# First routing group of a fused WKV-attention and mixture-of-experts kernel: temporaries in PSUM columns in place of SBUF, the mask of the two chosen experts by one comparison, the gates' products in two operations

## The chip, the cores and the metric

The kernel runs on one core of one Trainium2 chip. The metric is the device time of one execution in microseconds (us); lower is better. The kernel before takes 592.07 us, the median of 3 runs. TensorE is PE below (PEld are its weight loads), VectorE is DVE, ScalarE is ACT, GpSimd is POOL, and SP is the engine that issues most of the DMA transfers.

## The reference, cut to what matters

```python
# attention: r, k, v [4, 8, 768, 48]; a state of 48 x 48 for each head decays by w in each step
y[:, :, t] = einsum('bhd,bhde->bhe', rt, state + einsum('bhd,bhe->bhde', u * kt, vt))
state = w * state + einsum('bhd,bhe->bhde', kt, vt)
# x = y as [3072 tokens, 384]; mixture of experts, E = 8, F = 1024, two experts for each token
noisy = x @ w_gate + log1p(exp(x @ w_noise)) * noise
top2 = the two largest of the 8; top2_w = exp(top2_l - max); top2_w /= top2_w.sum(-1) + 1e-9
for e in range(8):
    mask = tokens that chose e
    out[mask] += top2_w * (relu(x[mask] @ w1[e]) @ w2[e])
```

## The kernel before, in words

The tokens are handled as 24 tiles of 128 (`NT`), tile i holding chunk i // 4 of batch i % 4. The first part of the kernel is a loop over these 24 tiles, `for i in range(NT)`. In each turn PE forms scores and outputs of tile i, DVE masks the next tile's scores (`mask`, L485), multiplies the transposed r by a table of powers (`rT`, L465), updates the state (`zt`, L508) and adds up the output tile x (`xout`, L561). PE then transposes x (L225 into `KX`), and ACT evicts that (`xT`, L471) for the product with the two gate matrices (L574). POOL multiplies k, r and u (L403, L422 and others), updates the state z (L512) and subtracts halves of the first expert's weights (L355, L358). SP issues all loads of r, k, v in order, five tiles ahead.

The second part is the experts, dense on PE: two products for each expert and chunk of tokens (L1136, L1172), with gathers and scatters by POOL.

Between them lies the routing, `route(g)`, once for each of two groups of 12 tiles (`GROUPS`). It computes from the logits `lg` the noise scale by a polynomial exponential (`expneg`) and a polynomial logarithm, finds the largest two of the 8 noisy logits (`m1`, `m2`, one-hot masks `oh`), sums the masks over the tokens by PE (`pr`, L819 to L822, with triangular and all-one matrices) to give each token its place in its expert's list, and builds the first expert's list by one-hot products (`pairs`, `drop`, `place`). The two gate weights come from a second, small `expneg` on the difference of the two logits (`r2` names) and from `gates()`; they are written to the DRAM rows `xd` beside x. All of it but the sums and products is DVE work on tiles of [128, 12, 8] (96 columns) or [128, 12] (12 columns).

The routing is written as generators. The attention loop takes a few of their steps in each turn (`steps(n)`), so that the routing of group 0 (tiles 0 to 11) stands in DVE's program between the attention operations of tiles 13 to 23, and that of group 1 after the loop. [...]

Where temporaries live: `T(name)` is a tile in SBUF. `P(k, shape)` is one of four columns of 96 in a tile `PG[0]`: for group 0 that is the PSUM tile `RT` (one bank of 512 columns), for group 1 the SBUF tile `PS`. `RT` also takes `pr` (columns from 384) and the lists' products (`drop`), and the third tile's transposes at the start of the experts (`xT_first`, columns 0 to 383, L1075), where PE leaves the loop: `xT_first` transposes three gathered tiles and the last x, and ACT and DVE split them into `xh` and `xl` for the first expert's products.

Of the kernel before, what the change touches and what calls it, by code (L numbers as in the profile page):

```python
# [56 lines left out]
def kernel(  # L57
# [14 lines left out]
    nc = tc.nc  # L72
# [513 lines left out]

    def expneg(a, shape, tg, res):

# [5 lines left out]
        r1, sc = T("r"), T("s", I32)  # L594
        t, nm, q = (P(k, shape) for k in (1, 2, 3)) if len(shape) == 3 else (T("t"), res, res)
        nc.vector.tensor_scalar(t, a, -LOG2E, MAGIC, op0=ALU.mult, op1=ALU.add)
# [26 lines left out]

    routed = set()

    def T_of(n):
# [28 lines left out]

    def pairs(g, sli, slf, nm):

        i0, i1 = GROUPS[g]
        shape = list(slf.shape)
        k = shape[1] if len(shape) == 3 else 1  # L660
        T = T_of(i1 - i0)
        ej = T(nm + "j", shape, I32)
        mm2, ej2 = T(nm + "m2", shape + [2], BF16), T(nm + "e2", shape + [2], BF16)
        nc.vector.tensor_single_scalar(ej, sli, 7, op=ALU.logical_shift_right)
        yield
        dup = [list(mm2.shape)] * 2
        ejb = (ej[:, :, None] if k == 1 else ej[:, :, :, None]).to_broadcast(dup[0])
        slb = (slf[:, :, None] if k == 1 else slf[:, :, :, None]).to_broadcast(dup[0])
        nc.vector.tensor_copy(ej2, ejb)
        yield  # L670
        nc.vector.scalar_tensor_tensor(mm2, ejb, -128.0, slb, op0=ALU.mult, op1=ALU.add)
        yield mm2, ej2
# [60 lines left out]

    GATES, list0 = {}, []

    def route(g, lists=True, behind=iter(())):
# [17 lines left out]
        for j, _ in enumerate(expneg(a, sh, "r1", ee)):  # L754
# [3 lines left out]
            yield  # L758
        d = rtp[0].tile([128, GB * E], F32, name="r1r", bufs=1)[:, :n * E].rearrange("p (a b) -> p a b", b=E)
        s, s2, q, nl, sn = T("s"), T("s2"), P(2, sh), T("nl"), T("sn")  # L760
# [22 lines left out]
        OHS[g] = oh  # L783
        da, e2 = T("da", [128, n]), T("e2", [128, n])
        if lists:
            m1, m2, nl2 = T("m1", [128, n, 1]), T("m2", [128, n, 1]), T("zp")
            nc.vector.tensor_reduce(m1, nl, AX.X, ALU.max)
# [8 lines left out]
            yield  # L796
            nc.vector.tensor_sub(da, m1[:, :, 0], m2[:, :, 0])
            yield
        else:
# [7 lines left out]
            nc.vector.tensor_sub(da, m8[:, :, 0], m8[:, :, 1])  # L807
        nc.vector.tensor_scalar(da, da, 87.0, None, op0=ALU.min)
        ex = expneg(da, [128, n], "r2", e2)
        yield  # L810
        om = T("om", dt=BF16)
        nc.vector.tensor_add(om, oh[:, 0], oh[:, 1])
        sm = rtp[0].tile([128, E, 1], F32, name="r_sm", bufs=1)
        yield
        nc.vector.tensor_reduce(sm, om.rearrange("p j e -> p e j"), AX.X, ALU.add)
        yield "pe"

        pr = RT[:, 4 * GB * E:(4 * GB + n) * E].rearrange("p (a b) -> p a b", b=E)
        nc.tensor.matmul(pr, ltri, om, start=True, stop=False, skip_group_check=True)  # L819
# [48 lines left out]
        if lists:  # L868
            s0, s0i = T("s0", [128, n]), T("s0i", [128, n], I32)
            nc.vector.scalar_tensor_tensor(s0, slf[:, :, 0], 1.0, om[:, :, 0], op0=ALU.add, op1=ALU.mult)  # L870
            yield
            nc.vector.tensor_scalar(s0i, s0, -1.0, None, op0=ALU.add)
            yield
            for c in pairs(g, s0i, s0i, "p"):
                yield 0.2
# [789 lines left out]
```

## Time and profile before

| | |
|---|---|
| runs | 592.07 us median of 3 (589.45, 592.07, 592.11) |
| profiled execution | 594.45 us, of which span of the instructions 592.3 us |
| PE busy | 570.7 us, 96% |
| DVE busy | 346.8 us, 59% |
| ACT busy | 284.8 us, 48% |
| POOL busy | 282.0 us, 48% |
| mean granted clock of PE | 0.991 |

The table is of one profiled execution; its time is 2.1 us more than its span, which is outside of the instructions. The shares are averages over two parts of the kernel: the attention loop lasts until about 127 us, the experts from there to the end.

### The profile page before, as it was taken

What the parts mean: (1) busy time and instruction counts of PE and PEld (TensorE: products, weight loads), DVE (VectorE), ACT (ScalarE), POOL (GpSimd) and SP (SyncE); (2) the same over time, 40 slices, a digit from 0 to 9 for tenths busy, and PEclk for the clock granted to TensorE, in tenths of its full rate; (3) what the DMA queues carried; (4) which work ended last, traced back from release to release, by engine and by line L of the source; (5) the groups of instructions that cost most, each with busy time, mean ns of one, the idle gap of its engine ahead of it and who ended that gap; (6) DMA issues with size and microseconds to landing.
All of it is one profiled execution on the core that took longest, in us unless ns stands there. A gap on an engine that the chain in (4) does not pass through costs nothing.

```text
span 592.3 us, 13907 instructions
## 1 busy us (share of the span) xinstructions
PE 570.7 (96%) x5383; PEld 544.7 (92%) x5384; DVE 346.8 (59%) x781; ACT 284.8 (48%) x714; POOL 282.0 (48%) x420
## 2 busy tenths in 40 slices
PE   8999989979979999999999999999999999999995
PEld 5899979869979999999999999999999999999995
DVE  7988889778745444546455645555464546454331
ACT  4348877832343443554445554455454454445220
POOL 8997767720426443436345443444353436333222
PEclk9999999989989999999999999999999999999998
DMA  8998999167504643675655646455756555424211
GB/s 162 196 210 190 232 224 233 54 168 225 157 2 140 208 145 92 177 181 146 122 166 142 191 107 185 120 178 111 177 132 152 150 149 171 128 92 85 66 35 42
DMA packets 143225, 86.53 MB, mean 146 GB/s; under 512 B 118624, under 2 KB 133215, under 8 KB 143152
## 3 DMA queue, kind: packets, MB, share of 16 engines
q1 hardware_dynamic: 132368, 56.76, 40.2%
q0 software_dynamic: 10160, 28.81, 16.3%
q8 instruction: 44, 0.72, 0.5%
q14 instruction: 29, 0.24, 0.1%
q10 hardware_dynamic: 624, 0.00, 0.1%
HBM read 58.81 MB, written 19.86 MB: 133 GB/s over the span
## 4 chain that ended last, share of the span: by engine, by line
PE 80%; DVE 7%; POOL 6%; issue 3%; ACT 2%; DMA 1%; another core or an unknown queue 1%; POOLq 0%; DVEq 0%; ACTq 0%
PE ph L1136 36%; PE pym L1172 33%; POOL kd L403 2%; PE pym L1165 2%; PE pym L1163 2%; POOL rku L411 2%; PE py L532 2%; DVE am L485 1%; POOL rku L415 1%; PE PAB L477 1%; DVE x L561 1%; PE KX L225 1%; DVE rT L465 1%; PE RT L714 1%; PE ptm L1054 1%
## 5 line engine op out<-in xcount | busy, mean ns | idle before, releaser
L1172 PE MATMUL pym<-w1h,hb 128*128 128x384 f32 x768 | 200.2, 337 | 0.0
L1142 DVE SCALAR_TENSOR_TENSOR hb<-ph,hb 128x384 fp32r<-128x384 f32 x128 | 71.2, 557 | 119.7 <-ACT ht L1140 73.6
L1172 PEld LDWEIGHTS pym<-w1h,hb 128*128 128x128 f32 x768 | 139.4, 188 | 0.2
L1136 PE MATMUL ph<-xh,w0h 128*128 128x384 f32 (+1 forms) x384 | 136.3, 355 | 0.0
L1136 PE MATMUL ph<-xh,w0l 128*128 128x384 f32 (+1 forms) x384 | 136.2, 355 | 0.0
L1136 PE MATMUL ph<-xl,w0h 128*128 128x384 f32 (+1 forms) x384 | 130.6, 354 | 0.0
L1172 PE MATMUL pym<-w1l,hb 128*128 128x384 f32 x384 | 129.2, 336 | 0.0
L1140 ACT ACTIVATE hb<-ph 128x384 fp32r<-128x384 f32 x128 | 62.9, 492 | 111.2 <-PE ph L1136 106.4
L1197 POOL DMA_INDIRECT out_dram<-ot,TK x56 | 60.0, 1071 | 100.4 <-DVE ot L1191 44.4
L1025 POOL DMA_INDIRECT xg<-xd,GR x56 | 60.9, 1088 | 53.6 <-DVE r_e L608 24.6
L1136 PEld LDWEIGHTS ph<-xh,w0h 128*128 128x128 f32 x384 | 72.9, 190 | 3.7 <-issue 0.2
L1136 PEld LDWEIGHTS ph<-xl,w0h 128*128 128x128 f32 x384 | 72.8, 190 | 3.3
L1136 PEld LDWEIGHTS ph<-xh,w0l 128*128 128x128 f32 x384 | 72.9, 190 | 3.2
L1040 POOL DMA_INDIRECT pv<-out_dram,GA x49 | 50.1, 1022 | 51.0 <-DMA out_dram<-ot,TK 38.6
L1172 PEld LDWEIGHTS pym<-w1l,hb 128*128 128x128 f32 x384 | 72.1, 188 | 0.1
L1110 ACT ACTIVATE xh<-xj 128x384 fp32r<-128x384 f32 (+1 forms) x42 | 21.2, 504 | 43.7 <-DVE xj L1108 38.3
L1180 ACT ACTIVATE ot<-pym 128x384 f32<-128x384 f32 x42 | 20.5, 487 | 41.3 <-PE pym L1172 31.7
L1111 DVE TENSOR_TENSOR xl<-xj,xh 128x384 fp32r<-128x384 f32 (+1 forms) x42 | 22.4, 534 | 24.9 <-ACT xh L1110 18.4
L1096 ACT ACTIVATE pl<-xg 128x768 uint16<-128x768 uint16 (+1 forms) x42 | 35.3, 841 | 1.6 <-DMA xd<-pl 1.5
L485 DVE TENSOR_TENSOR am<-PAB,mneg 128x512 int32<-128x512 int32 x48 | 30.8, 685 | 4.2 <-PE PAB L477 2.8
L454 ACT ACTIVATE cv<-vt,c 128x48 f32<-128x48 f32 x120 | 30.3, 326 | 0.2
L403 POOL TENSOR_TENSOR kd<-kt,tabk 128x192 f32<-128x192 f32 x46 | 28.6, 643 | 3.6 <-PE RV L225 2.4
(275 smaller groups left out, 828.2 us busy)
## 6 DMA issues: line engine op xcount, KB each, us to landing
stg<-in_moe_w_dram SPq DMA_DIRECT2D x24, 512.0 KB
stg<-in_moe_w_dram SPq DMA_DIRECT2D x32, 384.0 KB
xd<-x SPq DMA_DIRECT2D x24, 196.0 KB
rd<-in_r_dram SPq DMA_DIRECT2D x24, 192.0 KB
vt<-in_v_dram SPq DMA_DIRECT2D x24, 192.0 KB
out_dram<-ot SPq DMA_DIRECT2D x16, 288.0 KB
kt<-in_k_dram SPq DMA_DIRECT2D x23, 192.0 KB
xg<-xd,GR POOLq DMA_INDIRECT x56
```

The costliest lines, as they stand in the source:

```text
L403: nc.gpsimd.tensor_mul(KD[i][:, h], kt[i][:, h], tabk[:, h, :D])
L454: nc.scalar.activation(CV[i][:, h, :], vt[i][:, h, :], AF.Copy, scale=C8[i][:, h, :])
L485: nc.vector.tensor_tensor(am[:, :, h].bitcast(I32), pa[:, :, h].bitcast(I32), mneg[:, None].to_broadcast([128, 2, NP // 2, 128]), op=ALU.b ...
L1025: nc.gpsimd.indirect_dma_start(out=xg[:n, :XW if e else DM], out_offset=None, in_=xd[:rows_of(early_)], in_offset=bass.IndirectOffsetOnAxi ...
L1040: nc.gpsimd.indirect_dma_start(out=pv[:n], out_offset=None, in_=out, in_offset=bass.IndirectOffsetOnAxis(ap=GA[:n, e * NJ + t:e * NJ + t + ...
L1096: nc.scalar.activation(pl[:n], XG[e, t][:n, :DM].bitcast(U16).rearrange("p (d two) -> p two d", two=2), AF.Copy)
L1111: nc.vector.tensor_sub(xl, xj, xh.bitcast(F32))
L1136: nc.tensor.matmul(ph[:, :w_], a[:, d, fs], x[:, d, :w_], start=(j == 0), stop=(j == len(q) - 1))
L1140: nc.scalar.activation(h_[:, f, 0, :], ph[:, a:b], AF.Relu)
L1142: nc.vector.scalar_tensor_tensor(h_[:, f, 1, :], ph[:, a:b], 0.0, h_[:, f, 0, :].bitcast(F32), op0=ALU.max, op1=ALU.subtract)
L1172: nc.tensor.matmul(py, hb[:, f, a, hs], x[:, f, :], start=(j == 0), stop=(j == len(q) - 1))
L1197: st = nc.gpsimd.indirect_dma_start(out=out, out_offset=bass.IndirectOffsetOnAxis(ap=TK[:n, q:q + 1], axis=0), in_=ot[:n], in_offset=None, ...
```

## The change: what it does, and the diff

For group 0 alone (`own`), temporaries move from SBUF tiles to columns of the PSUM tile `RT`, through a new helper `V(c, shape)`: the reciprocal `d`, the noisy logits `nl`, the masked logits `nl2`, the difference `d0`, the small exponential's `et` and `e2`, the counts `sm`, the list's `s0`, `ej` and `ej2` (the last in four bytes in place of two). The prefix sums `pr` move to the columns 0 to 95, and `s0` is taken from `pr` itself. The mask of both chosen experts, `om`, is the comparison of `nl` with `m2` in place of the sum of the two one-hot masks. In `gates()` the two gate values are also kept in PSUM, which doubles the reciprocal and the product, and the products with the one-hot masks are two operations of 96 columns in place of one of 192. Group 1 is as before. Nothing else in the kernel is changed.

```diff
-    def expneg(a, shape, tg, res):
+    def expneg(a, shape, tg, res, t=None):
-        t, nm, q = (P(k, shape) for k in (1, 2, 3)) if len(shape) == 3 else (T("t"), res, res)
+        t, nm, q = (P(k, shape) for k in (1, 2, 3)) if len(shape) == 3 else (T("t") if t is None else t, res, res)
...
+    def V(c, shape, dt=F32):
...
+        t = RT[:, c:c + w_]
...
-    def pairs(g, sli, slf, nm):
+    def pairs(g, sli, slf, nm, pv=None):
-        ej = T(nm + "j", shape, I32)
-        mm2, ej2 = T(nm + "m2", shape + [2], BF16), T(nm + "e2", shape + [2], BF16)
+        ej = T(nm + "j", shape, I32) if pv is None else pv[0]
+        mm2 = T(nm + "m2", shape + [2], BF16)
+        ej2 = T(nm + "e2", shape + [2], BF16) if pv is None else V(pv[1], shape + [2])
...
+        own = lists and PG[0] is RT
+        d = P(1, sh) if own else rtp[0].tile(...)
...
+        if own:
+            nl = P(1, sh)
         nc.vector.tensor_add(nl, q, zp)
...
+        d0, e2, et = (V(4 * GB * E + j * GB, [128, n]) for j in range(3)) if own else (da, T("e2", [128, n]), None)
-            m1, m2, nl2 = T("m1", [128, n, 1]), T("m2", [128, n, 1]), T("zp")
+            m1, m2, nl2 = T("m1", [128, n, 1]), T("m2", [128, n, 1]), P(3, sh) if own else T("zp")
...
-            nc.vector.tensor_sub(da, m1[:, :, 0], m2[:, :, 0])
+            nc.vector.tensor_sub(d0, m1[:, :, 0], m2[:, :, 0])
...
-        nc.vector.tensor_scalar(da, da, 87.0, None, op0=ALU.min)
-        ex = expneg(da, [128, n], "r2", e2)
+        nc.vector.tensor_scalar(da, d0, 87.0, None, op0=ALU.min)
+        ex = expneg(da, [128, n], "r2", e2, et)
...
-        nc.vector.tensor_add(om, oh[:, 0], oh[:, 1])
-        sm = rtp[0].tile([128, E, 1], F32, name="r_sm", bufs=1)
+        if own:
+            nc.vector.tensor_tensor(om, nl, m2.to_broadcast(sh), op=ALU.is_ge)
+        else:
+            nc.vector.tensor_add(om, oh[:, 0], oh[:, 1])
+        sm = V(5 * GB * E + E + 2 * E, [128, E, 1]) if own else rtp[0].tile([128, E, 1], F32, name="r_sm", bufs=1)
...
-        pr = RT[:, 4 * GB * E:(4 * GB + n) * E].rearrange("p (a b) -> p a b", b=E)
+        po = 0 if own else 4 * GB * E
+        pr = RT[:, po:po + n * E].rearrange("p (a b) -> p a b", b=E)
...
+            if own:
+                gp = V(4 * GB * E + 2 * GB, [128, 2, n])
+                nc.vector.tensor_scalar(gp[:, 1], e2, 1.0, 1e-9, op0=ALU.add, op1=ALU.add)
+                yield
+                nc.vector.reciprocal(GTS[:, 0, i0:i1], gp[:, 1])
+                nc.vector.reciprocal(gp[:, 0], gp[:, 1])
+                yield
+                nc.vector.tensor_mul(GTS[:, 1, i0:i1], e2, GTS[:, 0, i0:i1])
+                nc.vector.tensor_mul(gp[:, 1], e2, GTS[:, 0, i0:i1])
+                yield
+                bc = [gp[:, kk, :, None].to_broadcast(sh) for kk in range(2)]
+                og, gd = T("os", [128, 2, n, E])[:, 0], T("a")
+                nc.vector.tensor_mul(og, oh[:, 0], bc[0])
+                yield
+                nc.vector.tensor_mul(P(2, sh), oh[:, 1], bc[1])
+                yield
+                nc.vector.tensor_add(gd, og, P(2, sh))
+                nc.sync.dma_start(xd[i0 * 128:i1 * 128, DM:].rearrange("(n p) e -> p n e", p=128), gd)
...
+                s0, s0i, pv = V(so, [128, n]), T("s0i", [128, n], I32), (V(so + GB, [128, n], I32), GB * E)
+                nc.vector.scalar_tensor_tensor(s0, pr[:, :, 0], 1.0, om[:, :, 0], op0=ALU.add, op1=ALU.mult)
```

No instruction changes its place among the others; what the edit moves is three added DVE instructions and some waits. The first place is DVE's program in the turn that follows PE's prefix sums (L596 is the first step of the small exponential, L485 the two halves of the mask of the next tile). Before:

```order
L465 TENSOR_TENSOR rT<-RV,pwr 128x2x4x64 [waits PE_49]
L596 TENSOR_SCALAR r2t<-r_da 128x12
L485 TENSOR_TENSOR am<-PAB,mneg 128x2x256 [waits PE_49]
L485 TENSOR_TENSOR am<-PAB,mneg 128x2x256
L598 TENSOR_SCALAR r_e_2127<-r2t 128x12 [waits DVE_49]
```

The same place of the change:

```order
L465 TENSOR_TENSOR rT<-RV,pwr 128x2x4x64 [waits PE_49]
L596 TENSOR_SCALAR RT<-r_da 128x12 [waits DVE_49,PE_49]
L485 TENSOR_TENSOR am<-PAB,mneg 128x2x256 x2
L598 TENSOR_SCALAR RT<-RT 128x12 [waits DVE_49]
```

L596 now waits for PE, since it writes the bank in which the prefix sums are formed, and the mask behind it has no wait of its own left. The second place is DVE's program at the last tile (x_149 is its x; behind it `gates()` ends, and `xT_first` begins). Before:

```order
L847 TENSOR_SCALAR GTS<-r_e_2127 128x12 [waits DVE_49]
L850 RECIPROCAL GTS<-GTS 128x12 [waits DVE_49]
L852 TENSOR_TENSOR GTS<-r_e_2127,GTS 128x12 [waits DVE_49]
L561 TENSOR_TENSOR x_149<-py,cv 128x384 [waits DMAHW4_49,PE_49,Activation_49]
L856 TENSOR_TENSOR r_os<-OH_242,GTS 128x192 [waits DVE_49]
L859 TENSOR_TENSOR r_a<-r_os 128x96 [waits DVE_49]
```

The same place of the change:

```order
L868 TENSOR_SCALAR RT<-RT 128x12 [waits DVE_49]
L870 RECIPROCAL GTS<-RT 128x12 [waits DVE_49]
L871 RECIPROCAL RT<-RT 128x12
L873 TENSOR_TENSOR GTS<-RT,GTS 128x12 [waits DVE_49]
L874 TENSOR_TENSOR RT<-RT,GTS 128x12
L561 TENSOR_TENSOR x_149<-py,cv 128x384 [waits DMAHW4_49,PE_49,Activation_49]
L878 TENSOR_TENSOR r_os<-OH_242,RT 128x96 [waits DVE_49]
L880 TENSOR_TENSOR RT<-OH_242,RT 128x96 [waits DVE_49]
L882 TENSOR_TENSOR r_a<-r_os,RT 128x96 [waits DVE_49]
```

Two instructions are new ahead of the last x, and one behind it. The third place is PE's program at the same point, the transposes of the third gathered tile into `RT` (L1075 before, L1121 of the change). Before:

```order
L225 MATMUL KX<-ident,x_149 128x64 x5
L1075 MATMUL RT<-ident,xg 128x128 [waits DMASW2_49]
L574 MATMUL pl<-wg,xT 64x64 [waits Activation_49]
```

The same place of the change:

```order
L225 MATMUL KX<-ident,x_149 128x64 x5
L1121 MATMUL RT<-ident,xg 128x128 [waits DMASW2_49,DVE_49]
L574 MATMUL pl<-wg,xT 64x64 [waits Activation_49]
```

The transposes wait for DVE as well now, since the gates' products lie in columns that they overwrite.

## Rows read from the trace of the kernel before

**Rows 1.** The page's first line.

```profile
span 592.3 us, 13907 instructions
```

**Rows 2.** Windows between PE's first product (L532) of one tile and the next.

```profile
core 0: us, PE busy (x) PEld busy (x) DVE busy (x) ACT busy (x) POOL busy (x), PEclk, DMA share, GB/s
...
77.45:82.93 5.48, 4.91 (x133) 4.63 (x131) 5.38 (x14) 3.92 (x13) 3.95 (x6) 1.00 0.81 175
82.93:89.53 6.60, 4.89 (x133) 4.64 (x130) 4.85 (x17) 4.51 (x16) 4.10 (x7) 1.00 0.99 244
89.53:95.31 5.78, 5.47 (x148) 5.12 (x144) 5.75 (x15) 4.30 (x15) 4.05 (x7) 1.00 0.99 230
95.31:100.03 4.72, 4.72 (x132) 4.60 (x130) 3.79 (x10) 3.60 (x13) 3.75 (x6) 1.00 1.05 224
100.03:106.02 5.99, 5.26 (x134) 4.79 (x131) 5.85 (x15) 4.11 (x15) 3.95 (x6) 1.00 0.68 186
106.02:111.25 5.23, 5.10 (x129) 4.67 (x127) 4.83 (x11) 5.08 (x19) 4.78 (x7) 1.00 0.22 80
120.79:127.65 6.86, 4.26 (x97) 3.51 (x93) 5.23 (x14) 4.33 (x15) 2.50 (x3) 1.00 0.40 115
```

**Rows 3.** Timeline of PE: starts, lengths, and the idle time ahead with its releaser.

```profile
82.59 0.40 PE L225 MATMUL KX<-ident,x 64*128 64x64 f32 x6 [0.57 <-DVE x L561]
...
88.07 0.41 PE L225 MATMUL RV<-ident,rd 64*128 64x64 f32 x7 [1.71 <-issue]
...
94.47 0.40 PE L225 MATMUL KX<-ident,x 64*128 64x64 f32 x6 [0.31 <-DVE x L561]
...
95.17 0.20 PE L822 MATMUL RT<-acc,ones_b 128*128 128x96 bf16 x1
...
96.74 0.62 PE L532 MATMUL py<-vt,am 128*64 128x48 f32 x16
...
105.69 0.40 PE L225 MATMUL KX<-ident,x 64*128 64x64 f32 x6 [0.61 <-DVE x L561]
...
125.79 0.40 PE L225 MATMUL KX<-ident,x 64*128 64x64 f32 x6 [1.10 <-DVE x L561]
126.12 0.55 PE L1075 MATMUL RT<-ident,xg 128*128 128x128 f32 x3
```

**Rows 4.** Timeline of DVE in group 0's routing.

```profile
80.38 1.13 DVE L765 TENSOR_TENSOR r_s<-r_nl,r1r 128x96 f32<-128x96 f32 x1
...
81.89 0.55 DVE L561 TENSOR_TENSOR x<-py,cv 128x384 f32<-128x384 f32 x1
...
92.62 0.77 DVE L808 TENSOR_SCALAR r_da<-r_da 128x12 f32<-128x12 f32 x1
...
100.35 0.74 DVE L870 SCALAR_TENSOR_TENSOR r_s<-SLF,r_om 128x12 f32<-128x12 f32 x1
...
123.21 1.15 DVE L608 SCALAR_TENSOR_TENSOR r_e<-r_e,r2r 128x12 f32<-128x12 f32 x2
```

**Rows 5.** Timeline of POOL at the same moments.

```profile
80.11 1.29 POOL L358 TENSOR_TENSOR w0l<-stg,w0h 128x512 fp32r<-128x512 f32 x1
...
92.36 1.00 POOL L358 TENSOR_TENSOR w1l<-stg,w1h 128x384 fp32r<-128x384 f32 x1
```

**Rows 6.** Timeline of DVE in group 1's routing, the same lines with POOL idle.

```profile
134.97 0.26 DVE L765 TENSOR_TENSOR r_s<-r_nl,r1r 128x96 f32<-128x96 f32 x1
...
140.64 0.17 DVE L808 TENSOR_SCALAR r_da<-r_da 128x12 f32<-128x12 f32 x1
```

**Rows 7.** DVE's groups by line and form: the same operation in PSUM and in SBUF.

```profile
L761 DVE TENSOR_SCALAR RT<-r_nl 128x96 f32<-128x96 f32 x1 | 0.3, 261 | 0.0
...
L761 DVE TENSOR_SCALAR PS<-r_nl 128x96 f32<-128x96 f32 x1 | 0.2, 211 | 0.0
```

**Rows 8.** Timeline of DVE at the last tile.

```profile
126.03 0.26 DVE L859 TENSOR_TENSOR r_a<-r_os 128x96 f32<-128x96 f32 x1
```

**Rows 9.** Timeline of ACT at the last tile.

```profile
126.96 0.52 ACT L1080 ACTIVATE xh<-RT 128x384 fp32r<-128x384 f32 x1
```

More of the change, by code (lines that the diff above doesn't have):

```diff
@@ L624 @@
     routed = set()
+    def V(c, shape, dt=F32):
+        w_ = 1
+        for z in shape[1:]:
+            w_ *= z
+        t = RT[:, c:c + w_]
+        t = t if dt == F32 else t.bitcast(dt)
+        ax = "abcd"[:len(shape) - 1]
+        return t if len(shape) == 2 else t.rearrange(f"p ({' '.join(ax)}) -> p {' '.join(ax)}",
+                                                     **dict(zip(ax, shape[1:])))
     def T_of(n):
@@ L732, in rest @@
             yield from drop(g, mm2[:, kk], ej2[:, kk], IJ_REST, (E - 1) * NJ, NJ, g == 0 and kk == 0)
-    GATES, list0 = {}, []
+    GATES, list0, gated = {}, [], []
     def route(g, lists=True, behind=iter(())):
@@ L758, in route @@
             yield
-        d = rtp[0].tile([128, GB * E], F32, name="r1r", bufs=1)[:, :n * E].rearrange("p (a b) -> p a b", b=E)
+        own = lists and PG[0] is RT
+        d = P(1, sh) if own else rtp[0].tile([128, GB * E], F32, name="r1r", bufs=1)[:, :n * E].rearrange(
+            "p (a b) -> p a b", b=E)
         s, s2, q, nl, sn = T("s"), T("s2"), P(2, sh), T("nl"), T("sn")
@@ L783, in route @@
         OHS[g] = oh
-        da, e2 = T("da", [128, n]), T("e2", [128, n])
+        da = T("da", [128, n])
+        d0, e2, et = (V(4 * GB * E + j * GB, [128, n]) for j in range(3)) if own else (da, T("e2", [128, n]), None)
         if lists:
-            m1, m2, nl2 = T("m1", [128, n, 1]), T("m2", [128, n, 1]), T("zp")
+            m1, m2, nl2 = T("m1", [128, n, 1]), T("m2", [128, n, 1]), P(3, sh) if own else T("zp")
             nc.vector.tensor_reduce(m1, nl, AX.X, ALU.max)
@@ L845, in gates @@
                 yield
+            if own:
[16 more added lines that the diff above has]
+                nc.sync.dma_start(xd[i0 * 128:i1 * 128, DM:].rearrange("(n p) e -> p n e", p=128), gd)
+                gated.append(g)
+                yield 0.25
+                return
             dn = GTS[:, 1, i0:i1]
@@ L868, in route @@
         if lists:
-            s0, s0i = T("s0", [128, n]), T("s0i", [128, n], I32)
-            nc.vector.scalar_tensor_tensor(s0, slf[:, :, 0], 1.0, om[:, :, 0], op0=ALU.add, op1=ALU.mult)
+            so = 4 * GB * E + 5 * GB
+            if own:
+                s0, s0i, pv = V(so, [128, n]), T("s0i", [128, n], I32), (V(so + GB, [128, n], I32), GB * E)
+                nc.vector.scalar_tensor_tensor(s0, pr[:, :, 0], 1.0, om[:, :, 0], op0=ALU.add, op1=ALU.mult)
+            else:
+                s0, s0i, pv = T("s0", [128, n]), T("s0i", [128, n], I32), None
+                nc.vector.scalar_tensor_tensor(s0, slf[:, :, 0], 1.0, om[:, :, 0], op0=ALU.add, op1=ALU.mult)
             yield
@@ L873, in route @@
             yield
-            for c in pairs(g, s0i, s0i, "p"):
+            for c in pairs(g, s0i, s0i, "p", pv):
                 yield 0.2
```

## The prediction

> **What bounds the kernel now.** I read the windows first, cut at PE's first product of each tile. The whole span is 592.3 us [rows 1], most of it experts that the edit does not touch. In the attention loop the turn from 95.31 to 100.03 us is one in which PE never waits: span and PE busy are both 4.72 us [rows 2]. I take that as the floor of a turn. The turns around it are longer although they hold the same attention work, and DVE is what is full there: 5.38 of 5.48 us, 5.75 of 5.78, 5.85 of 5.99 [rows 2]. These are the turns in which group 0's routing stands in DVE's program.
>
> Next the timeline of PE: in each of these turns it idles ahead of the transposes of x, and the releaser is DVE's x (L561): 0.57, 0.31 and 0.61 us, and 1.10 us at the last tile [rows 3]. One hole has another cause: 1.71 us at 88.07 us, where PE waited for nothing that the profile shows [rows 3].
>
> Last, DVE's own rows beside POOL's. L765 takes 1.13 us in group 0 [rows 4] and 0.26 us in group 1, where POOL is idle [rows 6]. It starts at 80.38 and ends at 81.51, and POOL's subtraction runs from 80.11 to 81.40 [rows 5]: DVE waits for POOL's operation to end and then does its own 0.2 us. L808 does the same (0.77 against 0.17 us [rows 4, 6]): it ends at 93.39, POOL's operation at 93.36 [rows 5]. So group 0's routing pays for a conflict with POOL, not for work. L765 has two inputs in SBUF; L808 has one, and goes from SBUF to SBUF.
>
> **The change, part by part.** I take it that an operand in PSUM takes such an operation out of the conflict: x (L561), which reads PSUM, takes 0.55 us while POOL works [rows 4]. I go by turns, since a turn can't fall under PE's floor; what DVE saves beyond that is lost. Moved operations that are not named in a turn (L835 and others) save time only where DVE is ahead of PE anyway.
>
> *Turn at 77.45 (L763, L765): 0.2 us.* The excess is 5.48 - 4.72 = 0.76 us, of which PE's wait for x is 0.57. L765 loses its stall of 1.13 - 0.26 = 0.87. But the next operation is s*s (L767), whose inputs stay in SBUF. It would now start at about 80.7, while POOL's subtraction still runs to 81.40 [rows 5], so it waits in place of L765. After it come about 0.26 us for L768 and x, which starts at about 81.65 in place of 81.89 [rows 4]. Bounds: nothing, and 0.57 if L767, which reads one tile twice, is free of the conflict. [...]
>
> *Turn at 89.53 (L791, L795, L808, the new mask): 0.45 us.* The excess over the floor is 5.78 - 4.72 = 1.06; the prefix sums, which stay, are some 0.5 of it (PE busy is 5.47 here), and PE's wait for x is 0.31 [rows 2, 3]. L808's 0.60 us alone is more than that wait. L797 still has two SBUF inputs and can still stall, but it has the rest of L808's and L791's savings to cover it. The comparison that makes the mask reads 96 columns at four bytes and is priced at L765's 0.26 us [rows 6]; x waits for PE's output by then. Bounds 0.31 and 0.56.
>
> *Turn at 95.31: 0.* It is at the floor. Here the new wait of L596 falls: it stands ahead of the mask (L485), and now holds it until the last prefix sum, which ended at 95.37 [rows 3]. Queued behind it are both halves of the mask, for which PE's output products wait; these began at 96.74, 1.37 us after the sums [rows 3]. L596 (12 columns, 0.17 as L808, [rows 6]) and the first half of the mask (I take x's 0.55, the row nearest in width, [rows 4]) need 0.7 to 0.8 with the start, so the cover is half a microsecond. If it were gone, the price would be what the mask comes late, up to the 0.5 that the sums take.
>
> *Turn at 100.03 (L870, L664, L669, L671): 1.15 us.* The excess is 5.99 - 4.72 = 1.27 us, PE's wait for x 0.61 [rows 2, 3]. L870 shows 0.74 us [rows 4] for 12 columns; group 1's 12-column L808 takes 0.17 [rows 6]. L870 stands ahead of the mask and so delays PE a second time. All four operations lose an SBUF input or output. Behind them L692 (two SBUF inputs, one of them the list's mask) stays and can stall once; I leave 0.1 for it. Bounds 0.61 and 1.27.
>
> *Turn at 106.02: 0.4 us.* PE does not wait for DVE's x here, but POOL waits for DVE's rT (L465) and PE for POOL's product. rT comes earlier when x does. Excess 5.23 - 4.72 = 0.51 us, PE idle 5.23 - 5.10 = 0.13 [rows 2]: bounds 0.1 and 0.51.
>
> *Last tile: 0.4 us.* The two steps of L608 ahead of x took 1.15 us [rows 4]. A 12-column operation alone takes 0.17 and a dependent one of 96 columns 0.26 [rows 6]; I take 0.28 for each step, so the pair saves 0.58. The second reciprocal and the second product are new ahead of x; nothing ahead of them holds them, so I charge each half of 0.17, together 0.17. That leaves 0.4 of PE's wait of 1.10 for x [rows 3]. Bounds: 0, and 0.8 (the stall down to two times 0.17, the new ones free). The new wait of L1121: the gates' last operation (L859) ended at 126.29 [rows 8], 0.5 us behind the start of x's transposes at 125.79 [rows 3]. With one operation more in front it is 0.6, the third tile's transposes start there in place of 126.12, take 0.55 [rows 3] and end at 126.94 on this clock; ACT, busy with what stands ahead, reads them at 126.96 [rows 9]. ACT's queue covers it with nothing to spare; without that cover it costs the 0.1 of the added operation.
>
> The move has a price of its own. L761 takes 261 ns into PSUM and 211 into SBUF [rows 7]; some 40 operations of group 0 move, 2.0 us if each costs 50 ns. I take nothing for it, since the turns at 89.53 to 106.02 leave DVE time once the stalls are gone, and the first and the last turn hold few moved operations.
>
> The sum: 0.2 + 0.45 + 1.15 + 0.4 + 0.4 = 2.6 us. Nothing behind 127 us changes except that it starts earlier. The span becomes 592.3 - 2.6 = 589.7, the profiled execution 594.45 - 2.6 = 591.85; that execution is 2.4 us over the median of the runs, so the median becomes 592.07 - 2.6 = 589.5 us, or 0.44% less. About 0.5% (2.96 us) is what a measurement of this kernel can tell from no change; the three runs themselves span 2.66 us.
>
> **The rivals.**
> *The stalls migrate.* L767, L797, both L692 and both L700 keep two SBUF inputs and take the waits over, as I have it for L767. For it: POOL is busy 3.7 to 4.8 us of each turn [rows 2], so a freed DVE meets it soon. Against it: x, not the routing, is what PE needs, and most of these stand behind PE's slack. The lower bounds add to 0 + 0.31 + 0.61 + 0.1 + 0 = 1.0 us: 591.0 us.
> *PSUM costs what it saves.* If the 2.0 us of the move were not hidden anywhere, 2.6 - 2.0 = 0.6 us would be left: 591.5 us. For it: L761's rows. Against it: DVE's saving in stalls is larger than the turns can use (L765, L808 and L870 alone lose 0.87 + 0.60 + 0.57), so there is room. [...]
> *PE's hole closes too.* The 1.71 us at 88.07 has no releaser, and the DMA share is 0.99 in that turn [rows 2, 3]; if it is a fetch of code that comes late among other transfers, other timing may remove it. With the upper bounds, 0.57 + 0.56 + 1.27 + 0.51 + 0.8 = 3.7, and 1.7 for the hole: 5.4 us, 586.7 us.
> *Such holes open elsewhere (slower).* The turns at 89.53 and 95.31 have DMA shares of 0.99 and 1.05. If a PE that no longer waits for x reaches the end of its code before it has landed, each could get a hole of 1.71: 3.4 - 2.6 = 0.8 us slower, 592.9 us. It decides once new holes are longer than 2.6 us. Against it: the turn at 95.31 ran at the floor with the highest share.
>
> **How the numbers follow.** My sum 0.52; migration 0.18; PSUM's price 0.05; the hole closes 0.17; new holes 0.08. The likeliest is the sum, 589.5. For the range I go from near the second rival's 586.7 to the migration's 591.0 and most of the way to 592.9, leaving out some 2 in 10: 587.0 to 591.8. The sum's own range is about half of the way to its bounds, 588.9 to 590.3. Faster by over 0.5% (under 589.1): the hole case 0.17 and somewhat under half of the sum's 0.52, together 0.41. Slower by over 0.5%: part of the last rival and what else may disturb a launch, 0.06. Within 0.5%: 0.53.
>
> **What would show it.** In the changed profile L870 and L808 of group 0 should be near 0.2 us, with L767 stalled to the end of POOL's subtraction; PE's waits for x in the turns of L791 and of L870 gone, and that in the turn of L765 still there; the turn behind the prefix sums still at 4.7 us; PE's transposes of the third tile without a wait over 0.2 us. I am wrong if the moved operations still take 0.5 us or more beside POOL, if the turns stay over 5.2 us with DVE idle, or if PE's holes without a releaser add up to something other than 1.7 to 2 us.

## The result, and the profile after

The changed kernel took 586.75 us, the median of 20 runs (584.44 to 594.04), beside 593.16 us for the kernel before (20 runs, 589.45 to 598.23). The medians lie 6.4 us apart. The ratio of the runs is 0.9908 with a 95% interval of 0.9887 to 0.9928: 5.4 us on 592, where I had forecast 2.6. Two later comparisons of the same two kernels read 0.9997 (0.9967 to 1.0027) and 0.9970 (0.9932 to 1.0009). The mean of the three is 0.9958, or 2.5 us, and the three lie further apart than their intervals allow. So the first comparison can't be read alone, and most of what follows is about which part of it is the change's.

The changed kernel's profiled execution took 584.44 us. Its first line answers to [rows 1]:

```profile
span 582.4 us, 13913 instructions
```

The windows between PE's first products of one tile and the next, for the same tiles as in [rows 2]:

```profile
core 0: us, PE busy (x) PEld busy (x) DVE busy (x) ACT busy (x) POOL busy (x), PEclk, DMA share, GB/s
78.97:84.05 5.08, 4.91 (x133) 4.65 (x131) 4.98 (x13) 3.90 (x13) 3.85 (x6) 1.00 0.78 170
84.05:89.56 5.51, 4.90 (x134) 4.64 (x131) 4.87 (x17) 4.50 (x16) 4.11 (x7) 1.00 0.90 216
89.56:94.98 5.42, 5.42 (x147) 5.15 (x143) 4.39 (x13) 4.41 (x15) 4.45 (x7) 1.00 0.85 185
94.98:99.87 4.89, 4.89 (x132) 4.69 (x130) 3.58 (x14) 3.67 (x14) 3.43 (x7) 1.00 0.94 225
99.87:104.56 4.69, 4.69 (x135) 4.57 (x131) 4.18 (x15) 4.09 (x15) 4.26 (x7) 1.00 0.99 232
104.56:109.35 4.79, 4.79 (x130) 4.62 (x127) 3.94 (x9) 4.67 (x18) 4.62 (x7) 1.00 0.79 238
117.54:122.98 5.44, 4.30 (x96) 3.51 (x93) 4.54 (x17) 4.33 (x15) 3.48 (x4) 1.00 0.61 184
```

From the third of these turns to the sixth PE is busy to the end, and DVE, which was full in two of these four before, has 0.5 to 1.3 us to spare in each. The lines of DVE that answer to [rows 4] stand 13 to 43 lines further down in the changed file (L778 was L765, L780 was L767, L807 was L791, L824 was L808, L913 was L870):

```profile
81.92 0.25 DVE L778 TENSOR_TENSOR r_s<-r_nl,RT 128x96 f32<-128x96 f32 x1
...
82.20 0.73 DVE L780 TENSOR_TENSOR r_s<-r_s 128x96 f32<-128x96 f32 x1
...
89.44 0.26 DVE L807 SCALAR_TENSOR_TENSOR RT<-OH,RT 128x96 f32<-128x96 bf16 x1
...
92.15 0.15 DVE L824 TENSOR_SCALAR r_da<-RT 128x12 f32<-128x12 f32 x1
...
95.09 0.17 DVE L596 TENSOR_SCALAR RT<-r_da 128x12 f32<-128x12 f32 x1 [0.94 <-PE RT L842]
...
99.75 0.18 DVE L913 SCALAR_TENSOR_TENSOR RT<-RT,r_om 128x12 f32<-128x12 f32 x1
...
118.68 0.38 DVE L608 SCALAR_TENSOR_TENSOR RT<-RT,r2r 128x12 f32<-128x12 f32 x2
```

and POOL beside the second of them:

```profile
81.55 1.27 POOL L358 TENSOR_TENSOR w0l<-stg,w0h 128x512 fp32r<-128x512 f32 x1
```

Of these rows each operation that now has an operand in PSUM takes what it takes without POOL: 0.25 us beside the 0.26 of L765 and 0.15 beside the 0.17 of L808 in group 1 [rows 6] (the last row is two steps). The square s*s, both of whose inputs are still in SBUF, ends at 82.93, and POOL's subtraction at 82.82: the stall moved there. On PE the hole of 1.71 us [rows 3] is 0.61 us, and the third tile's transposes wait 0.54 us:

```profile
88.10 0.40 PE L225 MATMUL RV<-ident,rd 64*128 64x64 f32 x7 [0.61 <-issue]
...
121.89 0.52 PE L1121 MATMUL RT<-ident,xg 128*128 128x128 f32 x3 [0.54 <-DVE xl L1128]
```

The two spans differ by 9.9 us, far more than the medians. Four pieces make it up: 3.7 us less from PE's first product at 71.66 (73.49 after) to that at 115.57 (113.66); 2.8 us less from there to the first product of the experts at 127.65 (122.98); 5.2 us less behind that; and 1.8 us more ahead of 71.66. The prediction speaks of the first piece and a part of the second only.

### The profile page after: what moved, and what is told of

It is laid out like the page before. It is cut to its first block, busy times and chain, and to the rows that moved or that the text cites. A ratio compares the mean times of both kernels' runs of the same rounds, so it can differ in the third digit from the quotient of the medians.

```text
span 582.4 us, 13913 instructions
## 1 busy us (share of the span) xinstructions
PE 568.3 (98%) x5383; PEld 542.7 (93%) x5384; DVE 340.6 (58%) x784; ACT 284.5 (49%) x714; POOL 279.1 (48%) x420
## 4 chain that ended last, share of the span: by engine, by line
PE 89%; DVE 5%; DMA 2%; issue 1%; POOL 1%; ACT 1%; POOLq 0%; DVEq 0%; ACTq 0%
PE ph L1182 37%; PE pym L1218 34%; PE py L532 4%; PE PAB L477 3%; PE pym L1211 2%; PE pym L1209 2%; DMA kt<-in_k_dram 2%; PE KX L225 1%; DVE am L485 1%; PE RV L225 1%; PE py L434 1%; PE py L574 1%; DVE cv L449 1%; PE RV L182 1%; PE ptm L1100 1%
## 5 line engine op out<-in xcount | busy, mean ns | idle before, releaser
L1071 POOL DMA_INDIRECT xg<-xd,GR x56 | 59.1, 1056 | 46.4 <-DVE r_e L608 21.5
L1226 ACT ACTIVATE ot<-pym 128x384 f32<-128x384 f32 x42 | 20.4, 486 | 40.6 <-PE pym L1218 32.9
L485 DVE TENSOR_TENSOR am<-PAB,mneg 128x512 int32<-128x512 int32 x48 | 30.9, 684 | 3.8 <-PE PAB L477 3.3
```

The costliest lines, as they stand in the source:

```text
L485: nc.vector.tensor_tensor(am[:, :, h].bitcast(I32), pa[:, :, h].bitcast(I32), mneg[:, None].to_broadcast([128, 2, NP // 2, 128]), op=ALU.b ...
L1071: nc.gpsimd.indirect_dma_start(out=xg[:n, :XW if e else DM], out_offset=None, in_=xd[:rows_of(early_)], in_offset=bass.IndirectOffsetOnAxi ...
```

## Two things in the trace that no edit here makes

**PE's signals.** In the trace of before, PE's products of the last tile but one end at 118.23, but DVE's copy (L443), which waits for them, starts at 119.69:

```profile
117.58 0.65 PE L532 MATMUL py<-vt,am 128*64 128x48 f32 x16
118.17 1.16 PE L477 MATMUL PAB<-rT,kT 64*128 64x128 f32 x16
119.69 0.17 DVE L443 COPY c<-py 128x8 f32<-128x8 f32 x1 [2.10 <-PE PAB L477]
```

In the trace of after the copy follows its products (they end at 116.34) by 0.04 us:

```profile
115.69 0.65 PE L532 MATMUL py<-vt,am 128*64 128x48 f32 x16
...
116.38 0.17 DVE L443 COPY c<-py 128x8 f32<-128x8 f32 x1 [0.70 <-PE py L532]
```

In before PE then waits 1.13 us for the x that comes late, and 1.01 and 1.10 us at the next two steps. I took this for the change's work at first.

**The granted clock.** The trace of before has PE at half of its full clock (0.50) from 128.0 to 131.3 us, at the start of the experts, and from 169.0 to 172.4, each behind waits of PE (the three above; 2.85 us near 169 us); the trace of after has it at the full clock until 580.5 of its 582.4 us. In the first stretch the products of 384 columns start 0.32 us apart, behind it 0.175. The expectations below call the half clock 1.2 GHz; what the rows give for it is 384 columns in 0.32 us, 1.20 a ns. Two windows of before, the start of the experts and the stage about 169 us (the clock is the third number from the end):

```profile
127.65:137.00 9.35, 9.35 (x48) 9.35 (x45) 7.63 (x29) 2.16 (x5) 0.00 (x0) 0.82 0.96 282
155.00:190.00 35.00, 32.04 (x202) 29.58 (x200) 20.06 (x62) 15.06 (x38) 13.72 (x18) 0.95 0.34 104
```

and the same two stages of after:

```profile
122.98:137.00 14.02, 14.02 (x89) 13.53 (x90) 12.26 (x46) 4.12 (x9) 0.00 (x0) 1.00 0.98 290
155.00:190.00 35.00, 34.79 (x206) 32.56 (x205) 18.89 (x52) 17.27 (x40) 18.19 (x24) 1.00 0.35 108
```

The theory I began with: removed stalls give some 2.5 us in the loop, and the shorter end of the loop keeps PE's clock up, which gives the rest. The rival: late signals and slow stretches come and go between executions and belong to no kernel.

## The experiments

One table holds what the traces of all of them say. "Eight turns" is from PE's first product (L532) at 71.66 in before to that at 115.57, and the same tiles in the others; "holes" is the sum of PE's waits of over 0.15 us in it that no releaser explains; then come the turns of L870 and of the tile behind it, the last two turns, and what is left of the span behind the experts' first product. Late: DVE's copy of the last tile but one starts over 1 us behind its products.

| kernel | eight turns | holes | L870 | next | last two | late | rest |
|---|---|---|---|---|---|---|---|
| before | 43.91 | 2.04 | 5.99 | 5.23 | 12.08 | yes | 464.7 |
| b_again | 42.25 | 2.20 | 5.54 | 5.22 | 12.11 | yes | 465.5 |
| w_before | 42.80 | 1.80 | 5.98 | 5.22 | 12.05 | yes | 463.7 |
| b_shift | 42.58 | 1.44 | 5.23 | 5.22 | 11.16 | no | 460.2 |
| e_logits | 41.71 | 1.05 | 5.54 | 5.23 | 12.46 | yes | 465.4 |
| e_exp | 44.78 | 2.56 | 5.70 | 5.23 | 12.88 | yes | 464.5 |
| e_list | 42.86 | 3.64 | 4.69 | 4.80 | 12.63 | yes | 464.7 |
| e_nologits | 40.25 | 1.00 | 4.69 | 4.80 | 11.40 | yes | 460.8 |
| after | 40.17 | 1.20 | 4.69 | 4.79 | 9.32 | no | 459.4 |
| a_again | 41.01 | 1.71 | 4.92 | 5.29 | 12.33 | yes | 465.4 |
| a_delay | 40.17 | 1.02 | 4.69 | 5.05 | 13.55 | yes | 465.0 |
| a_third | 41.09 | 1.70 | 4.68 | 4.79 | 11.39 | yes | 463.7 |
| a_shift | 40.41 | 0.62 | 4.68 | 4.81 | 11.48 | yes | 460.2 |
| a_trim | 44.15 | 3.18 | 4.69 | 5.60 | 12.08 | yes | 464.9 |

Two things account for what the last column ranges over. The first is a second place of late signals. In the twelve traces with late signals ACT stands for 2.2 to 3.8 us ahead of an eviction (hb) near 168 us, and PE then waits for group 1's list, which ACT has to make behind it; after and b_shift wait 0.3 us there. In before, ACT starts 2.8 us behind the product that it waits for (165.15 and 0.36), and PE stands for 2.85 us:

```profile
165.15 0.36 PE L1136 MATMUL ph<-xh,w0l 128*128 128x448 f32 x1
...
169.38 1.16 PE L714 MATMUL RT<-r_ob,r_oa 128*128 128x100 bf16 x12 [2.85 <-ACT r_ob L705]
```

```profile
168.29 0.49 ACT L1140 ACTIVATE hb<-ph 128x384 fp32r<-128x384 f32 x1 [3.02 <-remote]
```

PE's wait is 2.0 to 3.7 us in eleven of the twelve and 0.64 in a_shift; after and b_shift have none. The second thing is the stretches at half clock behind the experts' first product, in which a product of 384 columns takes 0.32 us in place of 0.175. With the wait and half of these stretches taken off (an estimate by the clock's 0.50), the rest lies between 457.9 and 459.5 us in all fourteen, with the change and without.

**b_again**, the kernel before once more.

> The kernel before, a second trace of it. Conflict and clock (my theory): the turns of DVE's stalls read as before to 0.15 us (5.48, 5.78, 4.72, 5.99, 5.23), the hole ahead of PE's transposes in the turn at 82.93 is there again (1.7 us), PE's last two turns add to over 11 us, and PE is granted 1.2 GHz for a stretch of over 2 us near 128 us. Chance of one execution (the rival): the stalls are there again, but the hole is under 0.8 us or the last two turns add to under 10 us or no stretch at 1.2 GHz lies near 128 us; then these pieces don't belong to the kernel and can't be gained from it. Time against itself 1.000.

Measured 0.9969 (0.9935 to 1.0003): a comparison of a kernel with itself can be off by 0.3%. L765 took 0.26 us this time, in place of 1.13; where POOL's subtraction stood then is not shown. L808 and L870 stalled as before (0.77 and 0.73 us). The hole at 88 us was gone, but four others added to 3.1 us, one of them ahead of the eight turns. The late signals stood at the same product, and the slow stretch came earlier, from 123.2 to 126.6.

**e_logits, e_exp, e_list**, one part of the change each. The prefix sums stand in the columns 0 to 95 in all three. The change is split by four flags:

```diff
         own = lists and PG[0] is RT
+        own_d, own_x, own_s, own_p = (own and z for z in (True, False, False, False))
-        d = P(1, sh) if own else ...
+        d = P(1, sh) if own_d else ...
```

> Of the change only the logits' part: the reciprocal, the noisy and the masked logits in PSUM, the mask by one comparison. Conflict by turns: L765's stall goes and L767 stalls in its place, turn at 77.45 shorter by 0.2 to 0.4; L795 and the mask help the turn at 89.53 by at most 0.3, since L808 still stalls: 0.5 us, ratio 0.999. If the hole at 88.07 closes because DVE runs ahead from L765 on, another 1.1 us: ratio 0.997. Clock theory: PE's idle time at the loop's end is as before, so the stretch at 1.2 GHz stays. Rival: the same as no change, 1.000, whatever the trace shows.

> Of the change only the small exponential and the gates in PSUM, with the new waits of L596 and L1121. Conflict by turns: L808 falls from 0.77 to 0.2 us (turn at 89.53 shorter by 0.3 to 0.4), the turn at 95.31 longer by 0.2 for L596's wait, the last tile 0.4 shorter, the late turns 0 to 0.5: 0.6 to 1.0 us, ratio 0.998. Clock theory: the two steps of L608 ahead of the last x and what follows are what leaves PE idle at the loop's end, so the stretch at 1.2 GHz near 128 us goes and the late signals with it: 3 to 4 us in all, ratio 0.994. Rival (chance): ratio 0.998, the stretch comes and goes without it.

> Of the change only the list's part: counts, s0, ej and ej2 in PSUM, s0 from the prefix sums themselves. Conflict by turns: L870 falls from 0.74 to 0.2 us, the turn at 100.03 is 1.0 to 1.3 us shorter, the turn at 106.02 some 0.3: 1.3 to 1.6 us, ratio 0.9975. Clock theory: nothing more, since PE's idle time at the loop's end is as before; the stretch at 1.2 GHz stays. If the three parts add up, the sum of the three gains is the change's 5.4 us (ratio 0.9908); if each alone gives its turns and the sum is under 4 us, something is gained only when all stalls are gone.

Measured 0.9975 (0.9940 to 1.0010), 0.9962 (0.9933 to 0.9990) and 0.9959 (0.9934 to 0.9985): none can be told from b_again. The rows can be told apart. In e_list alone the turns of L870 and behind it are short, by 0.5 to 1.3 and by 0.42 us. L808 keeps its stall there, to the end of POOL's operation (94.99 beside 94.96):

```profile
94.22 0.77 DVE L825 TENSOR_SCALAR r_da<-r_da 128x12 f32<-128x12 f32 x1
...
103.40 0.18 DVE L914 SCALAR_TENSOR_TENSOR RT<-RT,r_om 128x12 f32<-128x12 f32 x1
```

and loses it in e_exp, where the logits' operations keep theirs. In these kernels L825 is L808 of before, L914 its L870, L779 its L765, and L808 its L791:

```profile
81.31 1.07 DVE L779 TENSOR_TENSOR r_s<-r_nl,r1r 128x96 f32<-128x96 f32 x1
...
90.56 0.81 DVE L808 SCALAR_TENSOR_TENSOR r_zp<-OH,r_nl 128x96 f32<-128x96 bf16 x1
...
93.88 0.16 DVE L825 TENSOR_SCALAR r_da<-RT 128x12 f32<-128x12 f32 x1
```

So each operand ends its own operation's stall: L914 takes 0.18 us in e_list (0.74 in before), L825 0.16 in e_exp (0.77). All three show the late signals and the stretch at half clock; e_exp, which I expected to lose it, has it from 124.0 to 134.3 us, and another from 89.9 to 93.3, which is part of its 44.78 us.

**a_again**, the changed kernel once more.

> The changed kernel again, on the chip of these runs. The kernel before, traced twice, and three partial versions of the change all show the same end of the loop: from the last tile but one PE's signals come 1.4 us and more behind the products that carry them, PE waits three times about 1 us, and is granted 1.2 GHz for 3.4 us and more near 128 us. If that is what the change takes away (theory: most of the gain behind 111 us and the missing slow stretches belong to the whole change), this trace shows again no late signal, last two turns of 9.3 us together in place of 12.1, a mean clock of 0.996 or more, and a ratio near 0.991. If it was the luck of one execution (rival), the late signals and the stretch at 1.2 GHz are here too, the turns from 77 to 111 us are short all the same, and the ratio is 0.995 to 0.997.

Measured 0.9997 (0.9967 to 1.0027). The rival's case: eight turns of 41.0 us beside 40.2 in after, but late signals, PE at half clock from 122.8 to 129.6, and 465.4 us of rest. My theory of the clock fell here.

**w_before**, fillers in before:

```diff
+        if i == NT - 1:
+            warm(4, RV[:, 0])
         yout(i)
...
-            xT_first(lambda: turn_x(i))
+            xT_first(lambda: (warm(4, KX[:, 0]), turn_x(i)))
...
             scores(i + 1)
+            if i == NT - 2:
+                warm(4, RV[:, 0])
```

> The kernel before with 12 idle products of PE (four each, 0.85 us) put into the three places where it waits for the last two x and the xT between them; their results are overwritten. Nothing else changes. Clock theory: PE is no longer idle at the loop's end, the stretch at 1.2 GHz at the start of the experts goes, and with it 1.7 us: 0.997. If PE's late signals wait for PE to run dry, they now come 0.85 us later, x is later by that, and the time grows by up to 2.5 us: 1.004 with the clock's gain lost. Rival: the clock falls all the same, 1.000.

Measured 1.0029 (0.9994 to 1.0064). PE's clock stayed full (1.00) through the loop's end:

```profile
116.00:129.03 13.03, 12.46 (x225) 9.29 (x223) 8.90 (x27) 7.68 (x28) 6.48 (x7) 1.00 0.33 94
129.03:138.00 8.97, 8.97 (x55) 8.90 (x52) 7.72 (x30) 2.64 (x6) 0.00 (x0) 1.00 0.99 288
```

The rest is 1.0 us shorter than in before, but the time does not show it. (It is 1.8 us shorter than in b_again, whose stretch near 169 us was twice as long.) In spite of the idle products PE transposes x 2.18 us behind the end of the products of the last tile but one, 2.23 in before: the signals came no later, so they don't wait for PE to run dry.

**a_delay**, two copies ahead of the last x:

```diff
+        if i == NT - 1:
+            for _ in range(2):
+                nc.vector.tensor_copy(PS[:, :DM], PY[i].rearrange("p h d -> p (h d)"))
         xout(i)
```

> The changed kernel with two copies of a 128x384 tile on DVE (0.55 us each, their result unused) ahead of the last x: PE gets 1.1 us more of idle time at the loop's end, nothing else changes. Clock theory: PE is granted 1.2 GHz for 3.4 us at the start of the experts, which costs another 1.7 us: 2.8 us over the changed kernel of the same call (ratio 0.005 over its). Without the clock's part: 1.1 us, 0.002 over its.

Measured 1.0027 (0.9990 to 1.0064), 1.9 us over a_again by medians: between the two, and not to be settled, since a_again had a slow stretch itself.

**e_nologits**, the change without the logits' part (flags False, True, True, True).

> The change without the logits' part: the small exponential, the gates and the list in PSUM, the reciprocal, the noisy and masked logits and the mask as before. By turns it should have all of the change's gain but 0.5 us (turns of L765 and L791). If PE's late signals and the slow stretch go with the whole gain of DVE's time, it shows them gone and reads 0.992; if it shows them as its two parts alone do, 0.995.

Measured 0.9976 (0.9935 to 1.0017). Its eight turns are as short as after's (40.25), and although its signals are late, PE never fell to half clock before the end: 460.8 us of rest. Late signals and the clock are two things. Its turn of L791 is 5.96 us, beside 5.42 to 5.47 without holes with the whole change, which is the 0.5 us that I gave to the logits' part; its other turns made up for it.

**a_third, a_trim, a_shift**, beside one set of runs of before. The edits, for a_trim

```diff
-        ex = expneg(da, [128, n], "r2", e2, et)
+        ex = expneg(da, [128, n], "r2", e2)
...
-            if own:
-                gp = V(4 * GB * E + 2 * GB, [128, 2, n])
...
```

(the old `gates()` follows), and for a_shift

```diff
     warm(WARM0, RV[:, 0])
+    for _ in range(100):
+        nc.tensor.matmul(RV[:, 0, :2], wsrc, wsrc[:, :2], start=True, stop=True)
```

> The changed kernel a third time, with another sample of runs. Theory now: the change gives 2.3 to 2.6 us in the loop between 72 and 116 us (turns of the mask, of L870 and behind it) and nothing behind that; the rest of the first comparison was executions in which PE's signals came on time, and these belong to no kernel. Then the eight turns from the tenth to the eighteenth first product add to 40 to 41 us (42.3 to 43.9 before), and the ratio is 0.9955 to 0.997. If the change itself keeps the signals on time (rival), the ratio is 0.990 to 0.993 and many runs have a mean clock of 0.997 or more.

> The changed kernel with two of its parts taken back: the small exponential's first temporary in SBUF, so that L596 waits for PE no longer, and the gates as before, in SBUF, without the second reciprocal and product and without the wait of the third tile's transposes for DVE. If these two waits cost what their rows say, the turn of the masks' sums is 0.2 to 0.4 us shorter, and the last tile 0.3 to 0.7: ratio 0.001 under that of the changed kernel of this call, which the times can't settle but the turns can. Rival: the old gates meet POOL's subtraction at the last tile and lose it again.

> The changed kernel with 100 products of two columns at PE's start, results overwritten, which put 200 instructions (three quarters of a turn) ahead of everything on PE. PE's late signals have begun at the same product, the last of the last tile but one, in nine traces of ten. If the place hangs on how many instructions PE has been through, they now begin about three quarters of a turn earlier, behind the tile before it; if it hangs on what the program does there, they begin at the same product. Time: 2 to 6 us more at the start, nothing else.

Measured 0.9970 (0.9932 to 1.0009), 0.9985 (0.9954 to 1.0015) and 0.9920 (0.9890 to 0.9949). a_third has 41.1 us of turns, late signals, and medians of 591.73 beside 595.62: the theory's case by the turns and the interval. In a_trim L596 no longer waits, yet its turn is 5.10 us, and e_exp and e_nologits, where it waits, show 4.68: the wait is not what that turn pays for. The transposes wait no longer either, and that gave nothing: from the end of the last x to the experts' first product it takes 1.92 us in a_trim and in before, and 1.93 in a_third, where they wait 0.34 us. Where PE doesn't wait for DVE there, it waits for ACT's xT (0.33 us in a_trim, 0.49 in before). In a_shift the late signals begin at the same product, so in this trace the place does not hang on a count of instructions. It has the lowest ratio of the twelve, in spite of some 3 us lost at the start (the 100 products take 2.70 us): it has the fewest holes (0.62 us), and PE's wait for group 1's list is 0.64 us.

**b_shift**, the same 100 products in before.

> The kernel before with the same 100 products of two columns at PE's start (results overwritten), which cost 3.3 us there. With the change these 200 instructions left 0.6 us of holes without a releaser in place of 1.2 to 1.7, and read 0.992 in spite of their cost. If the holes hang on where PE's code is cut against the loads and not on the change, they are under 1 us here too, DVE's stalls stand as before (eight turns of 41 to 42 us, turns of L808 and L870 at 5.8 and 5.5 to 6.0 us), and the ratio is 0.996 to 1.000; the change is then worth 0.4 to 0.5% here as well. If the holes are the change's, they add to 2 us again and the ratio is 1.004 to 1.006.

Measured 0.9995 (0.9965 to 1.0025): the same products cost before nothing either, though some 3 us go at its start. Beside a_shift this is a fourth reading of the change, 0.9920 / 0.9995 = 0.9925 or 4.4 us, across two chips. Holes of 1.44 us lie between the two cases. Its trace is the second with signals in time:

```profile
119.65 0.65 PE L534 MATMUL py<-vt,am 128*64 128x48 f32 x16
120.23 1.16 PE L479 MATMUL PAB<-rT,kT 64*128 64x128 f32 x16
120.35 0.17 DVE L445 COPY c<-py 128x8 f32<-128x8 f32 x1 [0.70 <-PE py L534]
```

So neither state belongs to one kernel: the kernel before can have the signals in time, the changed kernel has them late in a_again and a_third, and with further edits in a_shift, a_delay and a_trim. Whether the change makes one of the two more frequent, two traces in time out of fourteen can't say.

## Why the prediction was right, and where it was off

The mechanism was right as far as the rows show it: group 0 paid for a conflict between DVE and POOL (L765 1.13 us, L808 0.77 and L870 0.74, while POOL works), with an operand in PSUM the same operations take 0.25, 0.15 and 0.18 us, and PE gets what it waited for. The x by which I took PSUM to be out of the conflict, at 81.89 [rows 4], stands where POOL is idle (81.40 to 83.21). The x of the turn behind it bears the step out, with 0.55 us beside a subtraction:

```profile
86.40 0.55 DVE L561 TENSOR_TENSOR x<-py,cv 128x384 f32<-128x384 f32 x1
```

```profile
86.18 0.99 POOL L355 TENSOR_TENSOR w1l<-stg,w1h 128x384 fp32r<-128x384 f32 x1
```

Over all traces the eight turns are 42.9 us on the mean of the four with before's code there (42.3 to 43.9) and 40.6 on that of the five with all of the change (40.2 to 41.1): 2.3 us, where my terms for these turns add to 2.2. That the two agree so well is in part luck. Of the 2.3 us, 1.45 lie in the four turns that I named. The other 0.9 lie almost all in the turns at 71.66 and 82.93, for which I had nothing and which hold most of the holes. With all holes taken off, the named turns give 1.7 us and the others nothing.

*Turn at 77.45, 0.2 us.* L767 took the stall over, as forecast: 0.46 to 0.84 us in all seven traces with the logits' part. Like L765, which stalled in [rows 4], it has two inputs in SBUF. What I took from one execution was the size of the stall: L765 showed 1.13, 0.26, 0.38 and 1.14 us in the four traces of before's code, and the turn's own length ranges over more than the change.

*Turn at 89.53, 0.45 us.* 0.36 in the first pair; without holes 5.61 to 5.78 before and 5.42 to 5.47 after where PE's code was not moved, 0.3 us. That is all that PE had to get: its busy time of 5.47 us is 0.75 over the floor, where I wrote 0.5 for the prefix sums, so that my own rows left 0.31. L808's stall is gone in every trace of the change.

*Turn at 95.31, 0.* It grew by 0.17 us in the first pair. L596 waited 0.94 us for the prefix sums as I had said, but a_trim clears it of the 0.17; without holes this turn is 4.71 to 4.94 us in the traces of before's code too, and what makes the difference stays open.

*Turns at 100.03 and 106.02, 1.15 and 0.4 us.* 1.30 and 0.44 in the first pair, 0.95 and 0.3 on the means of the same four and five traces; e_list shows that the list's part alone gives both.

*Last tile, 0.4 us.* Mis-sized: in traces with late signals and a full clock before the experts, the last two turns are 11.4 to 11.5 us with the change, and 12.1 without, 0.6 to 0.7 us. L608's pair went to 0.38 us, near my lower bound. The wait of the third tile's transposes, which I priced at 0 to 0.1, was 0.16 to 0.54 us, and at a full clock it cost what I had said: the time from the last x to the experts' first product is 1.92 us without it, and 1.93 and 2.00 in a_third and a_shift. In after it is 2.35, since there DVE's split of the second tile (L1128) stands ahead of the third's.

With signals in time, L608's pair cost more in before's code than I priced. In b_shift, where it is L610, it starts while POOL issues a gather and ends with the second of two subtractions:

```profile
122.65 2.71 DVE L610 SCALAR_TENSOR_TENSOR r_e<-r_e,r2r 128x12 f32<-128x12 f32 x2
```

```profile
122.38 0.95 POOL L1027 DMA_INDIRECT xg<-xd,GR  x1 [0.30 <-issue]
123.35 1.02 POOL L357 TENSOR_TENSOR w1l<-stg,w1h 128x384 fp32r<-128x384 f32 x1
124.30 1.01 POOL L360 TENSOR_TENSOR w1l<-stg,w1h 128x384 fp32r<-128x384 f32 x1
```

In after the pair takes 0.38 us beside the same gather, and the last two turns take 9.3 us in place of 11.2. How much of these 1.8 us is the stall's is not shown: in b_shift PE also waits for gathered rows until 126.44, 0.3 us short of x's end.

```profile
126.44 0.40 PE L227 MATMUL PAB<-ident,xg 64*128 64x64 f32 x6 [2.17 <-DMA xg<-xd,GR]
126.78 0.40 PE L227 MATMUL KX<-ident,x 64*128 64x64 f32 x6
```

*The price of PSUM* stayed hidden, and where the same operation can be compared it is smaller than the 50 ns of [rows 7]: 12 columns of L605 take 0.17 us from SBUF to SBUF (before) and into PSUM (after), and a step of L608 without a stall takes 0.16 to 0.17 us from SBUF and 0.17 to 0.18 from PSUM.

*The hole.* My third rival priced its closing at 1.7 us. That counted one hole of one execution: by the means of the same four and five traces, holes fell from 1.9 to 1.25 us. Nothing shows that this is the change's: the holes add to 0.6 to 1.7 us with it, to 1.4 to 2.2 without, and to 3.6 and 3.2 in e_list and a_trim, which have parts of it. My own sign of being wrong came here: in after they add to 1.20 us, not to 1.7 to 2. Another came in the turn at 89.53, which stays over 5.2 us with DVE idle for 1.0 us, though PE is busy throughout.

The sum by the traces: 2.3 us in the eight turns and 0.65 behind them, 2.9 us or 0.5%, beside a forecast of 2.6, and 2.3 us if the holes' part is left out. The three timed comparisons give 2.5 on the mean, but range from 0.2 to 5.4, so the times alone can't tell these sums apart. The 586.75 us of the first lie a quarter of a microsecond under my range; whether they need another mechanism of the change is not shown. Its runs came with a full clock far more often: 12 of 20 had a mean of 0.996 or more, 3 of 12 in a_third and none in a_again; of the 116 runs of before in the later comparisons, eight. Where both kernels had 0.997 or more on one chip, with a_third, three runs of before took 589.55 to 593.22 us (mean 591.8), and three of after 589.00 to 590.06 (589.4): 2.4 us. Why the first 20 runs were so often undisturbed is open.

Where the prediction was off is a step that I never wrote: I took the trace of before from 111 us on as fixed ("Nothing behind 127 us changes except that it starts earlier"). The last two turns and the rest range over 3.6 (a_delay left out) and 6.1 us from one trace to the next, more than the change, and the late signals and the clock make most of that.

## What to carry to other kernels

Here small operations of DVE took over four times as long beside POOL as alone (L765 1.13 us and 0.26, L808 0.77 and 0.17). An operand in PSUM ended that (0.25 and 0.15 us), and L767, which kept two inputs in SBUF, took L765's stall over (0.73 us in after). Where rows show such a pair of times, try an operand in PSUM, and look which operation behind it takes the stall over. What DVE saved was worth only what PE waited for in that turn: L808 lost 0.62 us, its turn 0.36. Before a gain under 1% is believed, trace the unchanged kernel twice and compare by stages; a stall, a hole or a slow clock that is not in both traces is not the edit's to win.

## What the runs showed of the hardware

**PE's holes follow packets of the instruction queue.** All 35 holes in the eight turns of the fourteen traces end 1.1 to 1.6 us behind the landing of a packet of that queue (q8, 16 KB): 1.53 and 1.24 us in before, 1.38, 1.31 and 1.31 in after. Most such packets (78 of 113 there) have no hole behind them, and what decides is open. Around the holes below, the packets of the data queue (q1) take 74 to 103% of the DMA engines' time. In before, for the hole that ends at 88.07, the DMA view of 85.5 to 86.9 us (queue, packets, MB, share of the engines) has it:

```profile
q1 hardware_dynamic: 1285, 0.25, 94.4%
q8 instruction: 1, 0.02, 5.4%
```

and that of 86.9 to 88.07 us has none of q8:

```profile
q1 hardware_dynamic: 1141, 0.24, 103.4%
```

e_exp (hole of 2.00 us to 89.22; q1 100.4%, then 74.2%) and a_third (1.16 us to 91.11; 95.9%, then 83.0%) show the same: one packet of q8 in the first window, none in the second. With 200 more instructions at PE's start the holes stand ahead of other products: 0.27 and 0.35 us in a_shift (91.26, 100.64) beside 0.42, 0.17 and 0.61 in after (77.71, 82.71, 88.10), and 0.82 and 0.62 us in b_shift (91.90, 101.60) beside 0.33 and 1.71 in before (76.18, 88.07).

**PE's late signals** begin at one product in 12 of 14 traces, some 1.5 us behind it (1.46 in before and e_list, 1.48 in b_again), and not at all in two (0.04 us in after, 0.05 in b_shift), of which after has the code of a_again and a_third. Near 168 us they are late again, by 2.78 us in before (165.51 to 168.29). No run here shows the cause.

**PE's clock** fell to half (0.50) at different moments (121.8 us in a_delay, 128.0 in before) behind the same waits, and stayed full (1.00) where 12 idle products filled them (w_before, 1.04 us each four); in e_nologits, a_third and a_shift it stayed up there without. In b_shift, with signals in time, it fell at 128.4 us behind a wait of 2.17 us for a DMA.
